# Routing of the first pair of batches moved behind GpSimd's last low part, and from GpSimd to VectorE

## The chip, the cores and the metric

The kernel runs on one core of a Trainium2 chip. The metric is the device time of one execution in microseconds (us); the median of several executions counts. PE is TensorE, DVE is VectorE, ACT is ScalarE, POOL is GpSimd, and SP issues most of the transfers.

## The reference

Three layers, in float32, one after the other:

```python
# attention: 4 batches, 8 heads, 576 positions, head size 64; each query sees itself and the 127 before it
scores = scale * q @ k.T  (masked to the window)  + slope[h] * -(i - j)
x = softmax(scores) @ v                               # -> 2304 tokens of 512
# mixture of 8 experts: each token goes to one
xn = x / (norm(x) + 1e-6);  en = emb / (norm(emb) + 1e-6)
logits = xn @ en.T / tau
expert = argmax(logits);  gate = softmax(logits)[expert]
x = gate * (relu(x @ w1[expert]) @ w2[expert])        # w1 512x1024, w2 1024x512
# dense layer, 512 -> 2048 -> 512, with a piecewise quadratic activation
out = g(x @ w_in) @ w_out
```

## The kernel before

The four batches are handled as two pairs (`pr` 0 and 1, `NP = 2`). A group `g` is one pair of batches and one pair of heads, eight in all (0 to 3 belong to the first pair of batches, 4 to 7 to the second); a group has nine units of 128 rows of queries, so the attention is 72 units. For a unit PE multiplies scores (`sc`, L862 to L867), DVE adds the bias and takes the maximum (`ss`, `mx`, L879), ACT takes the exponential (`at`, L887), PE transposes (`tp`, L894), ACT or DVE copies the transposed weights (`aT`, L899 or L901), and PE multiplies with the values (`av`, L914).

Queries and keys are split into a high part, made by ACT (`qs`, `kh`, L696 and L699), and a low part, made by DVE or POOL (`low`, L679; in groups 1 to 7 the planner chooses the engine). There are 16 splits, numbered 0 to 15, two to a group; PE's score matmuls need them.

Beside the attention run the steps of the routing. When the first pair's units are done, `route(0)` finds the expert of each token: the largest logit, its one-hot, running counts, the place of each token in its expert's list (`key`, `ki`, `lo`), then one-hots of these places in bf16 (`eqp`, `ocp`, `oap`, L403 to L412), which PE multiplies into the table of tokens (`tabp`, L420). From the table follow the expert that will be computed first (`efirst`), whose weights SP then loads (`wraw`), and its first token rows (`tabf`, L323), which POOL gathers from memory (`early_rows`, L565). `roots(0)` takes the root of the sums of squares of the first pair's tokens (`nsq` to `nrm`) by fifteen small operations after the two integer ones; on POOL before. `gates(0)` makes the gate weights from it (`inv`, L492, to `gfirst`, L323). With these ACT scales the gathered rows (L568), PE transposes them (`xpe`, L572), and they form the left side (`xte`) of the first expert's first 128 rows, which PE multiplies with unsplit weights (`hpe`, L1216) as soon as the attention ends. `route(1)` and `route(2)` do the same for the second pair.

The order of instructions on each engine is written by a planner when the program is built. Each step is a Python generator that yields an `ask`: the engines that could do it with assumed times, an earliest start, and names of events (`after`) that must have been seen. `drive` repeatedly takes the step with the earliest start on the planner's own clock. Events are kept in `seen` with planned times: `seen["split", n]` is the planned end of split `n`. An `after` moves a step in the order; it is no wait on the chip. There, each engine runs its instructions in the written order, and waits only for the data and buffers that an instruction uses. In planned idle time of PE the planner places small matmuls (`warm_up`, L815), whose results nobody reads. Arrival times of loads are planned by `arrival`.

After the attention come the experts (from L1455 on) and the dense layer, in which PE works without a break worth naming.

Of the kernel before, what the change touches and what calls it, by code (L numbers as in the profile page):

```python
# [15 lines left out]
ALU = mybir.AluOpType  # L16
# [4 lines left out]
P = 128  # L21
B, H, S, D = 4, 8, 576, 64
# [6 lines left out]
NT = 9  # L29
NP = B // 2  # L30
# [9 lines left out]
FILL, LEAST = 1.0, 0.45  # L40
TICK = 3.4133
EROOT = "G"
LATE = (0.4, 0.2, 0.5, 0.5, 0.2, 0.3)
OVER = (1, 3)
KEY = 4096
EVAC_DVE = (1, 3, 5, 7)
CT = CAP // P
# [13 lines left out]
def fused_kernel(ctx, tc, qk, vT, v, emb, tau, w1, w2, win64, wout64, out):  # L61
    nc = tc.nc
# [95 lines left out]
    seen, rings, work, held = {}, {}, {}, {}  # L158
    recent, warm, banks = [], [], []
    now, end, on, at_unit = [0.0], [0.0], ["", None], [0.0]  # L160

    def ask(engines, start=0.0, after=(), ring=None, late=None, duty=None, port=False):

        return engines, start, after, ring, late, duty, port
# [75 lines left out]
    def arrival(size):  # L240
        dma[0] = max(dma[0], end[0] + 0.65) + size / 0.35e6
        return dma[0] + 1.3

    rs_ = ExitStack()
    pr_ = rs_.enter_context(tc.tile_pool(name="pr", bufs=1, side="right"))
# [4 lines left out]
    nsq = pr_.tile([P, NQ], F32, name="nsq", bufs=1)  # L250
    nsq3 = pr_.tile([P, NQ], F32, name="nsq3", bufs=1)
    nrm = pr_.tile([P, NQ], F32, name="nrm", bufs=1)
# [78 lines left out]
    def vec(took=0.1, after=(), **k):  # L331

        return ask({"V": took}, end[0] + 0.13, after, port=True, **k)

    def of_tiles(what, c0, n):
        return [(what, q) for q in range(c0, c0 + n) if (q % NT) % 2 == 0]

    def route(i):
        c0, n = PARTS[i]
        pr, t0 = divmod(c0, NT)  # L340
# [4 lines left out]
        size = lambda m: 0.07 + m * n * E / 960  # L345
        lx = pr_.tile([P, n], F32, tag=f"lx{n}", name="lx")

        e, eng = ("V", nc.vector) if i else ("G", nc.gpsimd)
        yield ask({"V": size(1)} if i else {"G": 0.3}, after=of_tiles("lsum", c0, n) + ([] if i else [("enb", 1)]))
        if i == 0:  # L350

            eng.tensor_tensor(ls, ls, esc.rearrange("p (o e) -> p o e", o=1).to_broadcast(sh), op=ALU.mult)
            yield vec(size(1))
        nc.vector.tensor_reduce(lx, ls, axis=AX.X, op=ALU.max)
        if i == 0:
            seen["scaled"] = end[0]
# [4 lines left out]
        yield ask({e: size(1) if i else 0.15 + n * E / 474}, end[0] + 0.13, port=True)  # L361
        eng.tensor_tensor(fm, fm, wfirst[:, :n], op=ALU.mult)
        fl = pr_.tile([P, n], F32, tag=f"fl{n}", name="fl")
        yield vec(size(1))
        nc.vector.tensor_reduce(fl, fm, axis=AX.X, op=ALU.max)
        yield vec(size(1))
        nc.vector.tensor_tensor(oh[:, :, 1:], fm.rearrange("p t e -> p e t"),
# [31 lines left out]
        nc.vector.scalar_tensor_tensor(lo, ki, -float(P), key, op0=ALU.mult, op1=ALU.add)  # L399
        eq, oc, oa = eqp[:, t0:t0 + n], ocp[:, t0:t0 + n], oap[:, :, t0:t0 + n]  # L400
        ws = [P, n, NSLOT]
        yield ask({"V": size(CT)}, end[0], [("placed", 0)] if i else [])
        nc.vector.tensor_tensor(eq, slots(n, slotv), bc(ki, ws), op=ALU.is_equal)  # L403
        for t in range(n):
            yield ask({"V": 0.16}, end[0])
# [66 lines left out]
    def roots(pr):  # L472

        cols = slice(pr * NT, (pr + 1) * NT)
        e, eng = ("V", nc.vector) if pr else ("G", nc.gpsimd)
        yield ask({e: 0.08 if pr else 0.19}, after=of_tiles("squares", pr * NT, NT) + of_tiles("most squares", pr * NT, NT))
        eng.tensor_tensor(nsq[:, cols], nsq[:, cols], nsq3[:, cols], op=ALU.add)
        yield from root_steps(pr_, nrm[:, cols], nsq[:, cols], "p", e)
        seen["root", pr] = end[0] + 0.13

    def root_steps(pool_, out_, s_, nm, e):
        for n, _ in enumerate(root(pool_, out_, s_, nm, nc.vector if e == "V" else nc.gpsimd)):
            yield ask({"V": 0.08} if n < 2 or e == "V" else {"G": 0.19}, end[0] + 0.13, port=True)
# [94 lines left out]
    with ExitStack() as a:  # L578
# [38 lines left out]
        def qk_loads(n):  # L617
            g, b = divmod(n, 2)
            if n == 0:
                raw[0, 0] = new_raw()  # L620
                for c, cols in enumerate(CUT):
                    for x in range(2):
                        yield ask({"S": 0.45})
                        both = slice(2 * cols.start, 2 * cols.stop)
                        nc.sync.dma_start(raw[0, 0][:, x].rearrange("p h s -> p (h s)")[:, both],
                                          qk[0, 0, :, x].rearrange("p h s -> p (h s)")[:, both])
                        seen["qk"[x], 0, 0, c] = seen["qk"[x], 0, 1, c] = arrival(P * 8 * (cols.stop - cols.start) / 0.85)
                yield ask({"S": 0.45})
                nc.sync.dma_start(embt, emb)
                seen["emb"] = arrival(1e5) + 1.2  # L630
            else:
                yield ask({"S": 0.45}, after=[("loads", n - 1)] + ([("split", n - 3)] if n >= 3 else []))
                raw[g, b] = new_raw()
                pr, hp = divmod(g, H // 2)
                for x in range(2):
                    if x:
                        yield ask({"S": 0.45})
                    nc.sync.dma_start(raw[g, b][:, x], qk[2 * pr + b, hp, :, x])
                    seen["qk"[x], n] = arrival(P * 8 * S)
            seen["loads", n] = now[0]  # L640
# [109 lines left out]
        def prep_experts():  # L750

            esq = x_tiles[1][:E, 1]
            s_, g, y, t, o = (pa.tile([E, 1], F32, name=f"es{i}") for i in range(5))
            sub, e = (nc.vector, "V") if EROOT == "V" else (nc.gpsimd, "G")
            small = {e: 0.08 if e == "V" else 0.19}
            yield ask({"A": 0.52}, after=["emb"])
            nc.scalar.activation(esq, embt, AF.Square, accum_out=s_)
            yield ask({"V": 0.08}, end[0] + 0.2)
            nc.vector.tensor_scalar(y.bitcast(I32), s_.bitcast(I32), 1, None, op0=ALU.logical_shift_right)
            yield ask({"V": 0.08}, end[0] + 0.13)  # L760
            nc.vector.tensor_scalar(y.bitcast(I32), y.bitcast(I32), -1.0, 1597463007.0, op0=ALU.mult, op1=ALU.add)
            yield ask(small, end[0])
            sub.tensor_scalar(g, s_, -0.5, None, op0=ALU.mult)
            for _ in range(3):
                yield ask(small, end[0] + 0.13)
                sub.tensor_tensor(t, y, g, op=ALU.mult)
                yield ask(small, end[0] + 0.13)
                sub.tensor_tensor(t, t, y, op=ALU.mult)
                yield ask(small, end[0] + 0.13)
                sub.tensor_scalar(t, t, 1.5, None, op0=ALU.add)  # L770
                yield ask(small, end[0] + 0.13)
                sub.tensor_tensor(y, y, t, op=ALU.mult)
            yield ask(small, end[0] + 0.13)
            sub.tensor_scalar(y, y, s_, 1e-6, op0=ALU.mult, op1=ALU.add)
            yield ask(small, end[0] + 0.13, after=["tau"])
            sub.tensor_tensor(y, y, taut, op=ALU.mult)
            yield ask({"V": 0.08}, end[0] + 0.13)
            nc.vector.reciprocal(o, y)
            yield ask({"A": 0.2}, end[0] + 0.13)
            diag = pa.tile([E, E], F32, name="diag")  # L780
            nc.scalar.activation(diag, ident[:E, :E], AF.Copy, scale=o)
            ready = end[0] + 0.13
            yield ask({"P": 1.1}, ready, (), "xp", duty=0.1)
            etp = ps_x.tile([P, 5, E], F32, tag="xp", name="etp")
            for c in range(4):
                nc.tensor.matmul(etp[:, c], embt[:, c * P:(c + 1) * P], diag, start=True, stop=True)
            nc.tensor.matmul(etp[:, 4], one, diag, start=True, stop=True)
            yield ask({"V": 0.3}, end[0] + 0.2)
            for j in range(2):
                nc.vector.tensor_copy(enb[1][j * D:(j + 1) * D, :, j], etp[j * D:(j + 1) * D, :4])  # L790
            nc.vector.tensor_copy(esc, etp[:, 4])
            rings["xp"].append(end[0])
            seen["enb", 1] = end[0] + 0.13
# [126 lines left out]
        def finish(g, t, n, av, bank):  # L920
# [11 lines left out]
            if hp == H // 2 - 1:  # L932
                yield ask({"V": 0.2}, scaled, so_far("lpt"), late=LATE[0])
                nc.vector.tensor_reduce(lsum[:, q0:q0 + n], lpt[:, t:t + n].rearrange("p t h e -> p t e h"), axis=AX.X, op=ALU.add)
                seen["lsum", q0] = end[0] + 0.13
            xt = x_tiles[pr]
            yield ask({"V": 0.335, "A": 0.1 + 0.26 * n}, scaled, late=LATE[1])
            xo = xt[:, t:t + n, hp * P:(hp + 1) * P]
# [9 lines left out]
            if hp == H // 2 - 2:  # L948

                for i in range(n):  # L950
                    yield ask({"A": 0.59}, ready, so_far("xt"), late=LATE[2])
                    junk = p2.tile([P, 3 * P], BF16, tag="junk", name="junk", bufs=1)
                    nc.scalar.activation(junk, xt[:, t + i, :3 * P], AF.Square, accum_out=nsq3[:, q0 + i:q0 + i + 1])
                seen["most squares", q0] = end[0] + 0.13
            if hp == H // 2 - 1:
# [8 lines left out]
                for i in range(n):  # L964
                    yield ask({"A": 0.41}, ready, late=LATE[2] if pr == 0 else 0.0)
                    junk = p2.tile([P, 3 * P], BF16, tag="junk", name="junk", bufs=1)
# [689 lines left out]
```

## Time and profile before

| | |
|---|---|
| median of 3 runs | 828.44 us (828.44 to 829.73) |
| the profiled execution | 834.81 us, its span 833.1 us |
| granted TensorE clock, mean | 0.988 of full speed |
| busy: PE, DVE, ACT, POOL | 816.2, 518.8, 421.1, 141.0 us |
| instructions: PE, DVE, ACT, POOL | 5264, 1380, 881, 220 |
| end of the attention | about 175 us into the span |

A matmul counts as busy for as long as the records say that it is in the array, at the low clock for longer, and the placed matmuls without a reader count too. So PE's 98% is not all work: a stage can be shortened where PE is idle, where its clock is low, or where it runs such fill.

### The profile page before, as it was taken

The page shows a single profiled execution, that of the slowest core. Times are in us where ns is not written, and L with a number is a line of the kernel's source. Part 1 is how long each engine was busy: PE and PEld are TensorE (multiplying, and loading weights), DVE is VectorE, ACT ScalarE, POOL GpSimd, SP SyncE. Part 2 cuts the span into 40 slices and gives each one's busy share as a digit, 9 for nine tenths or more (in the row PEclk, how much of TensorE's full clock was granted, in tenths as well). Part 3 has the DMA queues.
Part 4 walks back from the last instruction along what each step waited for, and adds up shares of the span by engine and source line. Part 5 has one row for each costly group of instructions (what it writes and reads, how often), then busy time and mean ns, then how long its engine had stood idle before and what let it go on. Part 6 is the DMA issues. An engine that isn't in the chain of part 4 may idle for free.

```text
span 833.1 us, 14293 instructions
## 1 busy us (share of the span) xinstructions
PE 816.2 (98%) x5264; PEld 759.2 (91%) x5264; DVE 518.8 (62%) x1380; ACT 421.1 (51%) x881; POOL 141.0 (17%) x220
## 2 busy tenths in 40 slices
PE   8999998999999999999999999999999999999996
PEld 7999998987999999999999999999999999999995
DVE  6667785798666677787649999554434354334442
ACT  6878987765444376566435555333222233223222
POOL 3875856113101101100000000003000003001001
PEclk7999999899999999999999999999999999999999
DMA  8656956047746477678223343021000011001001
GB/s 297 239 184 228 335 221 233 27 144 220 238 137 193 149 268 251 225 246 260 73 67 134 119 137 113 1 77 76 1 1 1 1 39 76 1 1 39 1 1 38
DMA packets 59181, 106.04 MB, mean 127 GB/s; under 512 B 3942, under 2 KB 35686, under 8 KB 59104
## 3 DMA queue, kind: packets, MB, share of 16 engines
q1 hardware_dynamic: 55776, 95.15, 34.0%
q0 software_dynamic: 3328, 9.90, 3.4%
q8 instruction: 43, 0.70, 0.3%
q14 instruction: 34, 0.28, 0.1%
HBM read 90.42 MB, written 14.62 MB: 126 GB/s over the span
## 4 chain that ended last, share of the span: by engine, by line
issue 56%; PE 13%; POOL 2%; ACT 0%; POOLq 0%; DVE 0%
PE bh L1455 2%; POOL out L1581 2%; PE by L1444 2%; PE by L1446 2%; PE bh L1457 2%; PE by L1445 2%; PE bh L1456 2%; PE bx L1292 1%; POOL xg L1163 0%; POOL gap L1580 0%; PE permp L1382 0%; POOLq L1652 0%; ACT whi L552 0%; ACT yo L1494 0%; ACT xh L1284 0%
## 5 line engine op out<-in xcount | busy, mean ns | idle before, releaser
L1536 PE MATMUL ch<-yh,wc_0h 128*128 128x384 f32 x384 | 129.2, 336 | 0.0
L1538 PE MATMUL ch<-yh,wc_0l 128*128 128x384 f32 x384 | 129.1, 336 | 0.0
L1544 DVE SCALAR_TENSOR_TENSOR r<-r 128x384 f32<-128x384 f32 x96 | 53.4, 557 | 121.0 <-ACT r L1542 117.6
L1537 PE MATMUL ch<-yl,wc_0h 128*128 128x384 f32 x384 | 128.7, 335 | 0.0
L1542 ACT ACTIVATE r<-ch,halfc 128x384 f32<-128x384 f32 x96 | 55.3, 576 | 117.8 <-PE ch L1538 117.8
L1563 PE MATMUL o<-wc_1h,gl 128*128 128x512 f32 x288 | 113.3, 393 | 0.1
L1564 PE MATMUL o<-wc_1l,gh 128*128 128x512 f32 x288 | 113.3, 393 | 0.0
L1547 ACT ACTIVATE gh<-r 128x384 fp32r<-128x384 f32 x96 | 50.5, 526 | 123.4 <-DVE r L1546 123.4
L1562 PE MATMUL o<-wc_1h,gh 128*128 128x512 f32 x288 | 112.0, 389 | 0.0
L1581 POOL DMA_INDIRECT out<-ot,permu x18 | 17.5, 974 | 462.6 <-ACT ot L1576 459.6
L557 DVE TENSOR_TENSOR wlo<-wraw,whi 128x1024 fp32r<-128x1024 f32 x64 | 78.1, 1222 | 20.4 <-ACT whi L552 19.8
L1455 PE MATMUL bh<-xh,whi 128*128 128x256 f32 (+6 forms) x256 | 80.5, 314 | 0.4 <-issue 0.4
L1550 DVE TENSOR_TENSOR gl<-r,gh 128x384 fp32r<-128x384 f32 x96 | 53.4, 556 | 43.8 <-ACT gh L1547 42.6
L1445 PE MATMUL by<-hl,whi 128*128 128x256 f32 (+6 forms) x256 | 77.5, 303 | 1.9 <-DVE tmp L148 1.6
L1444 PE MATMUL by<-hh,whi 128*128 128x256 f32 (+6 forms) x256 | 77.5, 303 | 0.0
L1446 PE MATMUL by<-hh,wlo 128*128 128x256 f32 (+6 forms) x256 | 77.4, 303 | 0.0
L1457 PE MATMUL bh<-xh,wlo 128*128 128x256 f32 (+6 forms) x256 | 77.3, 302 | 0.0
L1456 PE MATMUL bh<-xl,whi 128*128 128x256 f32 (+6 forms) x256 | 77.1, 301 | 0.0
L1536 PEld LDWEIGHTS ch<-yh,wc_0h 128*128 128x128 f32 x384 | 72.1, 188 | 2.9 <-DVE r L1546 0.3
L1537 PEld LDWEIGHTS ch<-yl,wc_0h 128*128 128x128 f32 x384 | 72.1, 188 | 2.5
L1538 PEld LDWEIGHTS ch<-yh,wc_0l 128*128 128x128 f32 x384 | 72.0, 188 | 0.0
L887 ACT ACTIVATE at<-ss,mx 128x256 f32<-128x256 f32 (+1 forms) x144 | 60.1, 478 | 16.8 <-DVE mx L879 16.5
(277 smaller groups left out, 1748.6 us busy)
## 6 DMA issues: line engine op xcount, KB each, us to landing
wraw<-in_w SPq DMA_DIRECT2D x64, 512.0 KB, 4.4
rqk<-in_qk SPq DMA_DIRECT2D x30, 576.0 KB, 6.5
raw<-in_w_in SPq DMA_DIRECT2D x16, 512.0 KB
raw<-in_w_out SPq DMA_DIRECT2D x16, 512.0 KB, 4.6
vT<-in_vT SPq DMA_DIRECT2D x16, 288.0 KB
yl<-ysT SPq DMA_DIRECT2D x6, 768.0 KB, 5.9
x_dram<-xt SPq DMA_DIRECT2D x8, 512.0 KB, 6.5
vt<-in_v SPq DMA_DIRECT2D x8, 438.0 KB, 6.5
```

The source lines that it names most:

```text
L1444: nc.tensor.matmul(y, w2h[:, o], hh[:, :cap], start=(ff == 0), stop=False)
L1445: nc.tensor.matmul(y, w2h[:, o], hl[:, :cap], start=False, stop=False)
L1446: nc.tensor.matmul(y, w2l[:, o], hh[:, :cap], start=False, stop=(ff == 7))
L1455: nc.tensor.matmul(hp, w1h[:, o], xh[:, c, :cap], start=(c == 0), stop=False)
L1456: nc.tensor.matmul(hp, w1h[:, o], xl[:, c, :cap], start=False, stop=False)
L1457: nc.tensor.matmul(hp, w1l[:, o], xh[:, c, :cap], start=False, stop=(c == 3))
L1536: nc.tensor.matmul(hp, w1h[:, o], yh[:, c], start=(c == 0), stop=False)
L1537: nc.tensor.matmul(hp, w1h[:, o], yl[:, c], start=False, stop=False)
L1538: nc.tensor.matmul(hp, w1l[:, o], yh[:, c], start=False, stop=(c == 3))
L1562: nc.tensor.matmul(out_, gh[:, o], w2h, start=(ff == 0), stop=False)
L1563: nc.tensor.matmul(out_, gl[:, o], w2h, start=False, stop=False)
L1564: nc.tensor.matmul(out_, gh[:, o], w2l, start=False, stop=(ff == FF // P - 1))
```

## The change

The root of norms of the first pair runs on DVE, as that of the second pair does. The one-hots of `route(0)` and both `roots` may be planned only after `("split", 15)`, named `ALONE`, which is the planned end of the last low part. Where DVE takes up a result of POOL, the planner now leaves 1.0 us (`AFAR`) in place of 0.13 at three places. The planned arrival of the first group's loads is altered: without the factor 1/0.85, and 1.5 us later for the second of its two column halves (`c` is 0 or 1).

```diff
+AFAR = 1.0
...
+    ALONE = ("split", NP * H - 1)
+
     def route(i):
...
             eng.tensor_tensor(ls, ls, esc.rearrange("p (o e) -> p o e", o=1).to_broadcast(sh), op=ALU.mult)
-            yield vec(size(1))
+            yield ask({"V": size(1)}, end[0] + AFAR)
         nc.vector.tensor_reduce(lx, ls, axis=AX.X, op=ALU.max)
...
-        yield vec(size(1))
+        yield ask({"V": size(1)}, end[0] + (0.13 if i else AFAR))
         nc.vector.tensor_reduce(fl, fm, axis=AX.X, op=ALU.max)
...
-        yield ask({"V": size(CT)}, end[0], [("placed", 0)] if i else [])
+        yield ask({"V": size(CT)}, end[0], [("placed", 0) if i else ALONE])
         nc.vector.tensor_tensor(eq, slots(n, slotv), bc(ki, ws), op=ALU.is_equal)
...
     def roots(pr):
 
         cols = slice(pr * NT, (pr + 1) * NT)
-        e, eng = ("V", nc.vector) if pr else ("G", nc.gpsimd)
-        yield ask({e: 0.08 if pr else 0.19}, after=of_tiles("squares", pr * NT, NT) + of_tiles("most squares", pr * NT, NT))
-        eng.tensor_tensor(nsq[:, cols], nsq[:, cols], nsq3[:, cols], op=ALU.add)
-        yield from root_steps(pr_, nrm[:, cols], nsq[:, cols], "p", e)
+        yield ask({"V": 0.08}, after=of_tiles("squares", pr * NT, NT) + of_tiles("most squares", pr * NT, NT) + [ALONE])
+        nc.vector.tensor_tensor(nsq[:, cols], nsq[:, cols], nsq3[:, cols], op=ALU.add)
+        yield from root_steps(pr_, nrm[:, cols], nsq[:, cols], "p", "V")
         seen["root", pr] = end[0] + 0.13
...
-                        seen["qk"[x], 0, 0, c] = seen["qk"[x], 0, 1, c] = arrival(P * 8 * (cols.stop - cols.start) / 0.85)
+                        seen["qk"[x], 0, 0, c] = seen["qk"[x], 0, 1, c] = arrival(P * 8 * (cols.stop - cols.start)) + 1.5 * c
...
             sub.tensor_tensor(y, y, taut, op=ALU.mult)
-            yield ask({"V": 0.08}, end[0] + 0.13)
+            yield ask({"V": 0.08}, end[0] + AFAR)
             nc.vector.reciprocal(o, y)
```

Since the planner works from these numbers, the order moves in many places of the attention. Three of them follow; a line number of the changed kernel is 3 or 4 above that of the kernel before.

POOL, late in the attention, before the change: the gather of the first expert's rows stands ahead of the low parts of splits 14 and 15, and the sum of squares `nsq` and the first steps of the root behind them.

```order
L565 DMA xt_142<-x_dram,tabf 128x512
L679 TENSOR_TENSOR qs<-rqk,qs 64x512
L679 TENSOR_TENSOR kl<-rqk,kh 128x576
L679 TENSOR_TENSOR qs<-rqk,qs 64x512
L712 TENSOR_TENSOR qz_159<-rqk,qz_159 64x2x64
L679 TENSOR_TENSOR kl<-rqk,kh 128x576
L679 TENSOR_TENSOR qs<-rqk,qs 64x512
L679 TENSOR_TENSOR kl<-rqk,kh 128x576
L712 TENSOR_TENSOR qz_159<-rqk,qz_159 64x2x64
L679 TENSOR_TENSOR qs<-rqk,qs 64x512
L679 TENSOR_TENSOR kl<-rqk,kh 128x576
L477 TENSOR_TENSOR nsq<-nsq,nsq_102 128x9
```

The same low parts on POOL after the change, with what follows them.

```order
L682 TENSOR_TENSOR kl<-rqk,kh 128x576
L682 TENSOR_TENSOR qs<-rqk,qs 64x512
L682 TENSOR_TENSOR kl<-rqk,kh 128x576
L715 TENSOR_TENSOR qz_159<-rqk,qz_159 64x2x64
L568 DMA xt_142<-x_dram,tabf 128x512
L460 COPY oh_78<-cum_76 128x8
```

The gather has moved from ahead of these low parts to behind them, and nothing of the root is left on POOL.

DVE, late in the attention, before the change: the first integer step of the root (`rt_ip`), which takes POOL's `nsq`, stands among the maxima (`ss`, `mx`) of the units; the one-hots stand some eighty instructions earlier.

```order
L926 TENSOR_SCALAR rs<-av 128x4
L899 COPY aT<-tp 128x2x128
L928 RECIPROCAL rs<-rs 128x4
L879 ISA ss,mx<-sc,mb 128x256
L879 ISA mx 128x1
L124 TENSOR_SCALAR rt_ip<-nsq 128x9
```

DVE after the change, one unit later in the attention: the one-hots, and behind them the root in turn with the steps from the table.

```order
L902 COPY aT<-tp 128x512
L407 TENSOR_TENSOR eqp<-slotv,ki_all 128x216
L410 TENSOR_SCALAR ocp<-rowi,lo_all 128x128
L413 TENSOR_TENSOR oap<-eqp,tokhi 128x216
L410 TENSOR_SCALAR ocp<-rowi,lo_all 128x128
L416 TENSOR_SCALAR oap<-eqp,pid 128x216
L410 TENSOR_SCALAR ocp<-rowi,lo_all 128x128 x7
L929 TENSOR_SCALAR rs<-av 128x4
L480 TENSOR_TENSOR nsq<-nsq,nsq_102 128x9
L125 TENSOR_SCALAR rt_ip<-nsq 128x9
L931 RECIPROCAL rs<-rs 128x4
L127 TENSOR_SCALAR rt_yp<-rt_ip 128x9
```

What was spread over two places of the attention and over two engines now stands in one block on DVE, and no instruction in it takes a result of POOL.

DVE at the program's start, before the change: the low parts of the queries' second column half stand ahead of the first unit's maxima.

```order
L679 TENSOR_TENSOR kl<-rqk,kh 128x256 x2
L821 TENSOR_SCALAR mb<-rel 128x256
L679 TENSOR_TENSOR qs<-rqk,qs 64x256 x2
L879 ISA ss,mx<-sc,mb 128x128
L879 ISA mx 128x1
```

The same place after the change.

```order
L682 TENSOR_TENSOR kl<-rqk,kh 128x256 x2
L824 TENSOR_SCALAR mb<-rel 128x256 x2
L882 ISA ss,mx<-sc,mb 128x128
L882 ISA mx 128x1
L882 ISA ss,mx<-sc,mb 128x128
L882 ISA mx 128x1
L682 TENSOR_TENSOR qs<-rqk,qs 64x256
```

The first unit's maxima no longer stand behind the second column half.

## Rows read from the trace of the kernel before

**Rows 1.** Windows: length; busy PE, PEld, DVE, ACT, POOL; granted clock; DMA share, GB/s.
```profile
117.20:131.00 13.80, 13.52 (x137) 12.47 (x135) 11.45 (x58) 12.02 (x37) 4.39 (x5) 1.00 0.59 214
144.50:152.10 7.60, 7.60 (x42) 7.60 (x43) 4.25 (x20) 4.61 (x12) 3.09 (x14) 0.58 0.01 3
152.10:167.30 15.20, 15.14 (x161) 14.40 (x160) 12.35 (x67) 13.67 (x43) 0.00 (x0) 1.00 0.10 36
175.30:198.70 23.40, 21.32 (x138) 15.49 (x135) 21.55 (x97) 14.08 (x32) 8.71 (x8) 1.00 0.48 151
198.70:640.00 441.30, 439.79 (x2710) 415.64 (x2711) 294.43 (x541) 209.53 (x372) 21.32 (x29) 1.00 0.42 137
```

**Rows 2.** Timeline near 144 us: start, duration, engine, instruction, [idle before <-releaser].
```profile
143.59 0.21 POOL L477 TENSOR_TENSOR nsq<-nsq,nsq 128x9 f32<-128x9 f32 x1
143.84 0.17 DVE L124 TENSOR_SCALAR rt_ip<-nsq 128x9 int32<-128x9 int32 x1 [3.49 <-POOL nsq L477]
144.49 0.58 PE L866 MATMUL sc<-kh,qs 128*128 128x256 f32 x1 [3.44 <-DVE mx L879]
```

**Rows 3.** Timeline, 119 to 132 us: POOL, and the ACT instruction that it names.
```profile
119.18 1.52 POOL L679 TENSOR_TENSOR kl<-rqk,kh 128x576 fp32r<-128x576 f32 x1
126.49 1.24 POOL L565 DMA_INDIRECT xt<-x_dram,tabf  x1 [5.80 <-DVE tabf L323]
131.46 1.29 POOL L679 TENSOR_TENSOR qs<-rqk,qs 64x512 fp32r<-64x512 f32 x1 [3.73 <-ACT qs L696]
...
126.35 0.65 ACT L696 ACTIVATE qs<-rqk 128x512 fp32r<-128x512 f32 x1
```

**Rows 4.** Timeline of PE: ninth unit's eight score matmuls and what follows, at either clock.
```profile
124.96 0.36 PE L862 MATMUL sc<-kh,qz 128*128 128x256 f32 x1
125.98 1.90 PE L914 MATMUL av<-vt,aT 128*128 128x73 f32 x16
...
147.82 0.56 PE L862 MATMUL sc<-kh,qz 128*128 128x256 f32 x1
149.67 2.47 PE L914 MATMUL av<-vt,aT 128*128 128x73 f32 x16
```

**Rows 5.** Timeline, 119 to 127 us: DVE's one-hots and table, and PE beside them.
```profile
119.05 0.37 DVE L403 TENSOR_TENSOR eqp<-slotv,ki_all 128x216 bf16<-128x216 f32 x1
119.34 1.41 DVE L406 TENSOR_SCALAR ocp<-rowi,lo_all 128x128 bf16<-128x128 bf16 x1
122.03 0.72 DVE L406 TENSOR_SCALAR ocp<-rowi,lo_all 128x128 bf16<-128x128 bf16 x4
126.01 0.18 DVE L323 TENSOR_REDUCE tabf<-tm 128x3 uint32<-128x24 f32 x1
...
120.10 1.03 PE L815 MATMUL av<-warm 128*128 128x220 bf16 x9
121.70 1.32 PE L420 MATMUL tabp<-oap,ocp 128*128 128x24 bf16 x18
```

**Rows 6.** Timeline of the start, and a window of 1 us with the granted clock.
```profile
7.71 0.82 DVE L679 TENSOR_TENSOR qs<-rqk,qs 64x256 fp32r<-64x256 f32 x2 [1.63 <-ACT qs L696]
9.44 0.53 PE L894 MATMUL tp<-ident,at 128*128 128x128 f32 x2 [1.46 <-ACT at L887]
...
11.00:12.00 1.00, 1.00 (x8) 1.00 (x6) 0.54 (x2) 0.72 (x3) 0.00 (x0) 0.50 1.01 394
20.00:21.00 1.00, 0.94 (x5) 0.64 (x4) 1.00 (x2) 1.00 (x4) 0.00 (x0) 0.50 0.03 8
```

**Rows 7.** Timeline: second pair's root on DVE; first pair's gates; PE's transposes of early rows.
```profile
182.91 0.16 DVE L133 TENSOR_TENSOR rt_tp<-rt_tp,rt_yp 128x9 f32<-128x9 f32 x1
...
152.13 0.16 DVE L492 TENSOR_SCALAR inv<-nrm 128x9 f32<-128x9 f32 x1
161.37 0.18 DVE L323 TENSOR_REDUCE gfirst<-tm 128x3 f32<-128x24 f32 x1
...
162.68 0.60 PE L572 MATMUL xpe<-ident,xt 128*128 128x128 f32 x4
```

## The prediction

> **What bounds the kernel now.** I read the busy time by stage first, then the timeline of each engine wherever PE stands idle, runs fill or runs at the low clock. From 198.7 us on PE is busy for 439.79 of 441.3 us at full clock [rows 1], and the change touches nothing there but the names of tiles. So whatever the first 199 us gain or lose is carried to the end. In those, three losses of PE show.
>
> The largest stands at 144 us. DVE sits idle for 3.49 us in front of `rt_ip`, the first integer step of the first pair's root, until POOL has added the squares (`nsq`, 143.59); PE's next scores wait 3.44 us, since their banks are freed by DVE's maxima, which stand behind `rt_ip` [rows 2]. POOL was not slow at `nsq`; it was late, because the low parts of splits 14 and 15 stand ahead of it. And these were late because the gather of the early rows stands ahead of them: POOL waited 5.80 us for `tabf`, spent 1.24 us on the gather, and began the next low part only at 131.46. The wait of 3.73 us there is put down to ACT, but ACT's instruction began at 126.35 and took 0.65 us; what ended at 131.4 was, I take it, the gather's landing [rows 3].
>
> After that pause PE runs at the lower of its two levels. The stage from 144.5 to 152.1 us has a mean granted clock of 0.58 [rows 1], so about 0.42 / 0.5 of its 7.6 us, 6.4 us, at 1.2 GHz. Eight score matmuls take 1.85 us there (147.82 to 149.67), against 1.02 us at full clock (124.96 to 125.98) [rows 4].
>
> The second loss is at 119 us: the first bf16 one-hot takes 1.41 us, while four of its kind take 0.72 us together [rows 5]. It began while POOL worked at a low part (119.18, 1.52 us [rows 3]) and ended with it. PE is given 1.03 us of fill at this place [rows 5]. The third is at the start: PE idles 1.46 us before its first transposes, since the first maxima stand on DVE behind low parts whose data is still coming (1.63 us idle), and from 11 to 21 us the clock is at 0.50 [rows 6].
>
> **The change part by part.** The sum is made against the profiled execution, 834.81 us (span 833.1 and 1.7 around it). It lies 6.4 us above the median, and I carry the difference over to the median as it is.
>
> Pause at 144 us: no instruction of DVE's in this place takes a result of POOL any more, and the gather has left POOL's row ahead of the low parts. Minus 3.44 us. What is late next there is nothing that I see: PE has scores, transposes and values queued.
>
> Low clock behind it: at full clock the 6.4 us would take 6.4 x 1.02 / 1.85 = 3.5 us, a gain of 2.9. But ACT is busy for 4.61 us of this stage and DVE for 4.25 [rows 1]; 7.6 - 2.9 = 4.7 would leave ACT no gap. I take 2.4, with bounds of 0 (the clock falls for another reason) and 2.9.
>
> The stage from 117.2 to 131 us loses from PE the fill of 1.03 us, the table's matmuls of 1.32 us (which come back below) and 0.28 us of idle time, 2.6 us together. The order puts four fill matmuls into it, some 0.4 us by the nine in 1.03. ACT is busy for 12.02 of 13.8 us [rows 1], so that not over 1.8 can be had. I take 1.6, bounds 0.5 and 1.8.
>
> The block on DVE is the price. One-hots: from 119.05 to 122.75 us are 3.7 us; less 1.2 for the held one and 0.3 for a unit's own steps between them, 2.2 us. The steps from `table` to `tabf`: ten at about 0.17 (the last took 0.18 [rows 5]), 1.7 us. The root: twelve operations more than before, at 0.16 as those of the second pair [rows 7], 1.9 us. Together 5.8 us, put ahead of stage 152.1 to 167.3, in which DVE is busy for 12.35 of 15.2 us [rows 1] and so has 2.85 us free. About 3.0 us do not fit. The lower bound is 1.3: then all of it fits, since DVE has gaps in the stage ahead too (4.25 busy of 7.6), and PE alone has the table's 1.32 us more. The upper bound is 5.8, if nothing fits because the gaps are where DVE waits for PE. A part of this is a new wait: `nsq` on DVE needs ACT's last squares, and the table's steps and the next maxima are queued behind it. I take 3.0, nearest to the free time that the stage shows.
>
> That lateness goes no further by itself. Weights: SP reads `efirst` and issues six loads of 512 KB, which now start some 25 us later in the program; the stage 144.5 to 152.1 moves 3 GB/s and that to 167.3 moves 36 [rows 1], so that the path is free, and they are first used after 175 us. POOL's root steps were 3.09 us of work on an idle engine [rows 1], and their going gains nothing by itself. From 175.3 to 198.7 us DVE is busy for 21.55 of 23.4 us [rows 1]: the second pair's routing is its bound, with the same instructions as before, and it moves as a whole.
>
> The start: with the first maxima ahead of the second column half, most of the 1.46 us before PE's first transposes should go. I take 1.5. Bounds: a loss of 1 us, since the order has 31 short fill matmuls there instead of 39, and the clock could fall sooner; and a gain of 4.5, if PE stays at full clock through the ten us in which it now does not (10 x 0.45 by rows 4).
>
> The other two uses of `AFAR` and the rest of the reordering I cost at nothing: PE is at work nearly throughout there, and the planner puts other ready work in their place.
>
> Sum: -3.44 - 2.4 - 1.6 + 3.0 - 1.5 = -5.9 us, so 828.9 for a profiled execution and **822.5 us** for the median.
>
> **The rivals.**
>
> *The block does not fit.* DVE is the bound from 152 us on and the start gains nothing: -3.4 - 2.4 - 1.6 + 5.8 = -1.6, so 826.8 us. For it speaks that DVE's free 2.85 us are in pieces; against it that ACT (13.67 of 15.2 busy [rows 1]) sets many of these pieces and DVE can work ahead.
>
> *Slower: the gates come too late for the early rows.* Between `inv` (152.13) and `gfirst` (161.37, 0.18) lie 9.4 us [rows 7]. Ahead of `inv` now stand the one-hots, 2.2 us, and the root as a chain of fourteen steps, about 0.2 each with its hand-over, 2.8: 14.4 us from the block's start to `gfirst`. PE reaches the transposes of the early rows (162.68) 10.5 us after `inv` before the change; the order now has them two units later, 4 to 5 us at 175 us for 72 units, and the table's 1.3 ahead: about 16. So it is hidden by some 1.5 us, and turns when the block's 25 or so steps take 0.3 us in place of 0.2, 2.5 us more. Then ACT stands at the scaling of the early rows with the last units' exponentials behind it, PE waits in one piece, and its clock falls as at 144 us, 2.9. That is -1.6 + 2.5 + 2.9 = +3.8, so 832.2 us.
>
> *The low parts are not over when the one-hots come.* `ALONE` is an event on the planner's clock, and no wait on the chip. If POOL is still at splits 14 or 15, the change does not do what it says: each one-hot that meets a low part is held, by the first one's excess 1.41 - 0.18 = 1.2 us [rows 5]. Four meetings cost 4.9, -5.9 + 4.9 = -1.0, so 827.4 us. Against it: POOL was done at 143.6 with 9.5 us of waits around the gather [rows 3] that now go, and the block's place on DVE was reached at 152 us before. The Trainium skill (SBUF — State Buffer, "Who interferes with whom") has this as an exclusive lock on a port pair that VectorE and GpSimd share, held for a whole instruction, and counts VectorE operations with two SBUF inputs too. The held one-hot agrees. By that rule the root's steps on DVE, most of them with two SBUF inputs, could also be held, so that this rival could cost more than its four meetings; no row here shows such a step beside a low part.
>
> *The start gains its clock back.* 4.5 in place of 1.5: -8.9, so 819.5 us. For it: the maxima and the scores behind them come sooner, and the long run of fill at the start is planned among denser work. Against it: the loads still set the pace there, at 394 GB/s in the window at 11 us [rows 6].
>
> **How the numbers follow.** Forecast 0.52, block that does not fit 0.17, late gates 0.11, low parts not over 0.06, start at full clock 0.14. About 0.2%, 1.7 us, can be told from no change; the cases at 826.8 and 827.4 lie at that bound, and I count about half of each as no difference. Faster: 0.52 + 0.14 + half of 0.23, less some, 0.77; within 0.2%: 0.12; slower: 0.11. The forecast by itself spans 819.5 to 825.5. Range: 818 us (start at full clock and a block that mostly fits) to 828.5 (both cases near no change), which leaves out the late gates and little else.
>
> **What would show it.** Right: no wait of DVE for POOL in the last third of the attention; PE's clock at full from 130 to 175 us; the nine bf16 one-hots all near 0.2 us; POOL's last low part ahead of the one-hots; DVE near full from the one-hots to 199 us. The experts' unbroken stage, from 198.7 us on before, begins some 6 us earlier. Wrong: a wait of ACT for `gfirst` or of PE for the gates' matmuls of more than 1 us, a low clock near 160 us, a one-hot over 1 us, or a low clock at the start that lasts longer than the ten us of now.

## The result, and the profile after

The changed kernel takes **822.19 us** (median of 5 executions, 822.14 to 824.10), the kernel before beside it 829.73 (828.44 to 831.86): ratio 0.9912, 95% interval 0.9889 to 0.9936. Measured a second time (after_again, below) it is 0.9917 (0.9900 to 0.9934). So some 7 us less (7.5 between the medians, 6.9 by the second ratio), with 5.9 predicted, and inside the range.

The profiled execution of after takes 822.19, its span 820.5. That of before was 834.81, which turned out to be the slowest of some 60 executions of that kernel. So the two traces differ by 12.6 us and the medians by 7.5, and the difference has to be told apart by stage.

Windows of the changed kernel, with the columns of [rows 1]. The first covers the stage that had the low clock in [rows 6], the fourth the stage that had it in [rows 1].

```profile
10.00:20.00 10.00, 9.91 (x88) 9.48 (x87) 8.52 (x34) 8.71 (x21) 3.07 (x4) 1.00 1.03 407
20.00:30.00 10.00, 9.39 (x82) 9.00 (x80) 8.27 (x38) 9.83 (x23) 9.36 (x12) 1.00 0.85 327
117.20:131.00 13.80, 13.53 (x128) 13.00 (x127) 7.54 (x42) 12.52 (x35) 7.66 (x7) 1.00 0.10 31
140.00:150.00 10.00, 10.00 (x97) 9.55 (x97) 8.82 (x64) 9.46 (x32) 1.22 (x1) 1.00 0.55 184
150.00:160.00 10.00, 9.15 (x96) 8.32 (x96) 8.25 (x41) 9.01 (x27) 0.00 (x0) 1.00 0.58 210
160.00:170.00 10.00, 9.32 (x71) 7.74 (x71) 9.35 (x43) 8.76 (x31) 0.21 (x1) 1.00 0.56 190
187.40:640.00 452.60, 451.50 (x2775) 426.59 (x2776) 299.52 (x552) 212.56 (x379) 21.32 (x29) 1.00 0.42 134
```

The clock is at full in all of these windows. PE has gaps from 150 to 170 us, 1.5 us together, while the tail of the block is worked off. From 187.4 us on it is busy for 451.50 of 452.60 us, as before from 198.7 on.

Timeline of the changed kernel: PE's start, then POOL, DVE, ACT and PE around the block.

```profile
8.12 0.44 PE L897 MATMUL tp<-ident,at 128*128 128x128 f32 x2
11.26 0.36 PE L869 MATMUL sc<-kh,qs 128*128 128x256 f32 x1
...
120.30 1.28 POOL L682 TENSOR_TENSOR qs<-rqk,qs 64x512 fp32r<-64x512 f32 x1 [5.49 <-ACT qs L699]
133.36 1.44 POOL L682 TENSOR_TENSOR kl<-rqk,kh 128x576 fp32r<-128x576 f32 x1
136.53 0.46 POOL L715 TENSOR_TENSOR qz<-rqk,qz 64x128 fp32r<-64x128 f32 x1 [1.73 <-ACT qz L713]
143.77 1.22 POOL L568 DMA_INDIRECT xt<-x_dram,tabf  x1 [6.78 <-issue]
...
136.64 0.59 DVE L407 TENSOR_TENSOR eqp<-slotv,ki_all 128x216 bf16<-128x216 f32 x1
137.96 1.22 DVE L410 TENSOR_SCALAR ocp<-rowi,lo_all 128x128 bf16<-128x128 bf16 x7
139.17 0.16 DVE L480 TENSOR_TENSOR nsq<-nsq,nsq 128x9 f32<-128x9 f32 x1
144.31 0.16 DVE L495 TENSOR_SCALAR inv<-nrm 128x9 f32<-128x9 f32 x1
152.80 0.18 DVE L324 TENSOR_REDUCE gfirst<-tm 128x3 f32<-128x24 f32 x1
...
153.01 0.72 ACT L571 ACTIVATE xt<-xt,gfirst 128x512 f32<-128x512 f32 x1 [0.22 <-DVE gfirst L324]
153.82 0.62 PE L575 MATMUL xpe<-ident,xt 128*128 128x128 f32 x4
```

POOL's last long low part ends at 134.8, and only a short one (`qz`, to 136.99) meets the block; before, `nsq` could begin behind the last one only at 143.59 [rows 2]. No one-hot is held (seven in 1.22, against the 1.41 of one in [rows 5]); `nsq` stands behind them without a wait; ACT waits 0.22 for `gfirst`.

To compare executions by stage, four marks are read from each PE timeline: the first score of the ninth unit of group 0 (`sc<-kh,qz`), the same of group 5, the experts' first `bh` matmul (some 6 us ahead of their unbroken stage), and the span's end. The runs below are in this table; "old" and "new" say which order PE's instructions have up to the first mark.

| kernel | order of the start | to ninth unit, group 0 | to that of group 5 | to `bh` | to the end |
|---|---|---|---|---|---|
| before | old | 27.69 | 97.27 | 68.15 | 639.99 |
| start_only | new | 22.07 | 97.57 | 67.85 | 638.81 |
| root_dve | old | 25.84 | 97.36 | 64.14 | 638.66 |
| gather_late | old | 24.18 | 97.41 | 63.58 | 639.33 |
| gather_late_start | new | 22.08 | 97.30 | 62.63 | 638.89 |
| gather_late_after | new | 21.66 | 97.32 | 62.93 | 638.99 |
| onehots_late | old | 22.64 | 96.89 | 62.38 | 638.99 |
| start_old | old | 23.09 | 96.84 | 63.00 | 638.97 |
| root_pool_late | new | 21.84 | 97.04 | 62.55 | 639.77 |
| after | new | 21.86 | 97.02 | 62.97 | 638.65 |
| after_again | new | 21.15 | 96.98 | 63.01 | 638.96 |
| afar_old | new | 21.55 | 97.00 | 63.01 | 638.54 |
| pause_fill | old | 22.62 | 98.78 | 64.38 | 639.12 |
| onehots_twice | new | 22.32 | 96.99 | 66.61 | 639.28 |

Between the profiled executions of before and after, 5.8 us lie ahead of the first mark, 0.2 in the second column, 5.2 in the third and 1.3 in the last.

### The profile page after: what moved, and what is told of

The parts are those of the page before. It is cut to its first block, busy times and chain, and to the rows that moved or that the text cites. A ratio compares the mean times of both kernels' runs of the same rounds, so it can differ in the third digit from the quotient of the medians.

```text
span 820.5 us, 14256 instructions
## 1 busy us (share of the span) xinstructions
PE 806.9 (98%) x5242; PEld 749.8 (91%) x5242; DVE 516.9 (63%) x1390; ACT 421.5 (51%) x881; POOL 137.7 (17%) x205
## 4 chain that ended last, share of the span: by engine, by line
issue 56%; PE 12%; POOL 2%; ACT 0%; DVE 0%; POOLq 0%; ACTq 0%
PE bh L1458 2%; POOL out L1584 2%; PE bh L1460 2%; PE bh L1459 2%; PE by L1447 2%; PE by L1449 2%; PE by L1448 2%; PE bx L1295 1%; ACT whi L555 0%; DVE wlo L560 0%; POOL gap L1583 0%; PE permp L1385 0%; POOLq L1655 0%; POOL xg L1166 0%; ACT yo L1497 0%
## 5 line engine op out<-in xcount | busy, mean ns | idle before, releaser
L555 ACT ACTIVATE whi<-wraw 128x1024 fp32r<-128x1024 f32 x64 | 67.3, 1055 | 0.7 <-ACTq L1476 0.7
```

## The experiments

Each ratio is to the kernel before on the same chip (medians there 829.4 to 829.9), with its 95% interval. Two theories stood against each other after the result: that the late part gives 4.4 us and the start 1.5, as the prediction sums it, or that the start gives 4.5 to 6.

### The start apart from the rest

start_only takes the kernel before and this line of the change alone; start_old takes the changed kernel and undoes it.

```diff
-                        seen["qk"[x], 0, 0, c] = seen["qk"[x], 0, 1, c] = arrival(P * 8 * (cols.stop - cols.start) / 0.85)
+                        seen["qk"[x], 0, 0, c] = seen["qk"[x], 0, 1, c] = arrival(P * 8 * (cols.stop - cols.start)) + 1.5 * c
```

> The kernel before with the planned arrivals of the first loads alone changed; the routing stays as it was. Theory A (the sum of the prediction: the start is worth the idle time of 1.46 us): 1.5 us less than before, 829.7 to 828.2, ratio 0.998, and the ten us at the clock's lower level stay. Theory B (the changed kernel's trace read after the fact: the start gains its clock back): PE at full clock from 10 to 20 us, where before has 0.55, and 4.5 to 6 us less, ratio 0.993 to 0.995. Both expect the pause of about 3.4 us in front of the root's first integer step to stay.

> The changed kernel with the old planned arrivals of the first loads; the rest of the change stays. Theory A (the start is worth 1.5 us, the late part of the attention 4.4): 823.7, ratio to before 0.993, low clock again from 10 to 20 us. Theory B (the start is worth 4.5 to 6 us of the 7.5 that the medians differ by): 826.7 to 828, ratio 0.996 to 0.998. Both expect no wait of VectorE for GpSimd and full clock from 130 to 160 us.

start_only: **0.9985** (0.9976 to 0.9994), 827.97 us. start_old: **0.9935** (0.9921 to 0.9948), 823.49 us. Theory A holds in the times: 1.2 us for the start (1.6 between the medians), 5.4 for the rest. It is wrong on the low clock, which is not there in either trace; theory B has the clock of start_only right and the price wrong. Windows of start_only, start_old and root_dve (below), in this order; the last two have PE's old order at the start:

```profile
10.00:20.00 10.00, 9.91 (x89) 9.48 (x88) 8.61 (x32) 8.69 (x20) 3.34 (x4) 1.00 1.02 395
```
```profile
10.00:20.00 10.00, 9.72 (x89) 9.40 (x88) 8.19 (x29) 8.41 (x21) 3.01 (x4) 1.00 0.97 368
```
```profile
10.00:20.00 10.00, 9.94 (x61) 9.30 (x62) 6.67 (x22) 7.01 (x19) 0.47 (x2) 0.66 0.87 349
```

One order of instructions shows 1.00 in one execution, 0.66 in another, and 0.55 in the profiled one of before. PE's idle time ahead of its first transposes was 0.39, 0.88 and 1.46 us in these three. Over all six profiled executions with the old order the first mark lies between 22.62 and 27.69, over the eight with the new one between 21.15 and 22.32. So the low clock there belongs to some executions of the old order and not to all: it shows in three of the six, in none of the eight.

The pause stands as before in start_only, and the clock behind it is low; timeline, and a window:

```profile
138.53 0.17 DVE L124 TENSOR_SCALAR rt_ip<-nsq 128x9 int32<-128x9 int32 x1 [3.48 <-POOL nsq L477]
139.19 0.58 PE L866 MATMUL sc<-kh,qs 128*128 128x256 f32 x1 [3.43 <-DVE mx L879]
...
137.50:144.00 6.50, 4.81 (x23) 4.82 (x24) 3.39 (x16) 3.22 (x8) 4.07 (x16) 0.55 0.01 3
```

### The root on VectorE alone

root_dve: the kernel before, with the first pair's root on VectorE and no event to wait for.

```diff
-        e, eng = ("V", nc.vector) if pr else ("G", nc.gpsimd)
+        e, eng = "V", nc.vector
```

> The kernel before with the first pair's root on VectorE and nothing else: no event to wait for, the one-hots early, the gather still ahead of the last low parts on GpSimd. Theory W (what cost time was VectorE's wait for GpSimd's result): the pause of 3.44 us goes, the clock stays full from 140 to 160 us (2.4 us), up to 1.9 us of added steps come back: 4 to 5.8 us less, ratio 0.993 to 0.995. Rival L (two engines on one port): GpSimd is at low parts until 143.6 us, beside the root's steps on VectorE; each step that meets one is held for up to 1.2 us, so that three or four holds take the place of the pause and the clock falls again: within 1 us of before or slower, ratio 0.999 to 1.003, with single root steps above 1 us in place of 0.16.

**0.9969** (0.9953 to 0.9984), 826.89 us: 2.6 less, between the two. Timeline:

```profile
138.53 0.27 DVE L477 TENSOR_TENSOR nsq<-nsq,nsq 128x9 f32<-128x9 f32 x1
139.35 1.24 DVE L126 TENSOR_SCALAR rt_yp<-rt_ip 128x9 int32<-128x9 int32 x1
140.84 1.25 DVE L128 TENSOR_SCALAR rt_ip<-nsq 128x9 f32<-128x9 f32 x1
...
139.28 1.28 POOL L679 TENSOR_TENSOR qs<-rqk,qs 64x512 fp32r<-64x512 f32 x1
140.64 1.42 POOL L679 TENSOR_TENSOR kl<-rqk,kh 128x576 fp32r<-128x576 f32 x1
```

The pause is gone, and two steps of nine columns stand until the low part beside them ends: 1.2 us each in place of 0.17. The clock stays at 1.00. Both theories hold in part: taking DVE off POOL's result helps, and doing so while POOL is still late costs up to 2.2 us of it.

### One-hots late, root left on GpSimd; and the gather alone

onehots_late: the kernel before with `ALONE` ahead of the one-hots only. The gather takes its rows from the table that these make, so it moves behind the low parts with them (in the trace it starts at 145.51, the last low part at 137.20).

```diff
-        yield ask({"V": size(CT)}, end[0], [("placed", 0)] if i else [])
+        yield ask({"V": size(CT)}, end[0], [("placed", 0) if i else ALONE])
```

gather_late: the kernel before with the gather in `early_rows` behind the last low part, and nothing else; gather_late_start: that and the new arrivals.

```diff
-        yield ask({"G": 1.1}, after=["first rows", ("squares", 0), ("most squares", 0)] + of_tiles("out", 0, NT))
+        yield ask({"G": 1.1}, after=["first rows", ("squares", 0), ("most squares", 0), ("split", NP * H - 1)] + of_tiles("out", 0, NT))
```

> The kernel before with the event ahead of the first pair's one-hots alone; the root stays on GpSimd, which now has it right behind the low parts, and the gather behind that. Theory Q (GpSimd was late because of its queue, the gather ahead of the low parts): no wait of over 1 us for the sum of squares though it is still made by GpSimd, full clock from 130 to 160 us; 3.44 + 2.4 + 1.6 less, and 3.9 of one-hots and table steps against 2.85 free, 1.1 more: 6.3 us less, ratio 0.992. Rival H (the hand-over between the two engines is what costs): VectorE waits for GpSimd at the integer steps or at the inverse norms for 2 us and more, or one-hots beside GpSimd's root are held for over 1 us: 2 to 3 us less at the most, ratio 0.996 to 1.000.

> The kernel before with one thing changed: the gather of the first expert's rows is planned behind the last low part. One-hots early, root on GpSimd, start as before. Theory Q (the whole late gain is GpSimd's queue: the gather ahead of the low parts): pause 3.44 and low clock 2.4 go, nothing comes back on VectorE: 829.6 less 5.8, 823.8, ratio 0.993, no wait above 1 us for the sum of squares, full clock from 130 to 160 us. Rival O (the one-hots' place matters as much: the first one is held beside a low part, and PE runs fill there): at least 1.6 us less of the gain, 825.4 or more, ratio 0.995 and above.

> The kernel before with two edits: the gather planned behind the last low part, and the new arrivals of the first loads. One-hots early, root on GpSimd, no longer distance where VectorE takes up a result of GpSimd. Theory Q (these two are the whole change): 0.993 x 0.9985 = 0.9915, 822.8, as the changed kernel. Rival O (the late one-hots or the longer distance carry a part): 1 us or more above the changed kernel, 823.7 or more, ratio 0.993 and above.

onehots_late: **0.9934** (0.9921 to 0.9947), 823.17 us: 5.5 less, nearer to the 6.3 of its theory Q than to the 3 at most of rival H. gather_late: **0.9930** (0.9912 to 0.9948), 824.30. gather_late_start: **0.9935** (0.9920 to 0.9950), 823.32. Theory Q holds for gather_late: the edit to one line of `early_rows` gives 5.8 us (4.3 to 7.3 by the interval), as much as the late part of the change (5.4 by start_old), with the one-hots early and the root on POOL. Timeline of gather_late:

```profile
123.62 1.27 POOL L679 TENSOR_TENSOR qs<-rqk,qs 64x512 fp32r<-64x512 f32 x1 [6.46 <-ACT qs L696]
137.10 1.44 POOL L679 TENSOR_TENSOR kl<-rqk,kh 128x576 fp32r<-128x576 f32 x1
138.73 1.24 POOL L565 DMA_INDIRECT xt<-x_dram,tabf  x1 [0.19 <-DVE mx L879]
143.38 0.20 POOL L477 TENSOR_TENSOR nsq<-nsq,nsq 128x9 f32<-128x9 f32 x1 [3.41 <-ACT junk L967]
...
143.61 0.17 DVE L124 TENSOR_SCALAR rt_ip<-nsq 128x9 int32<-128x9 int32 x1
```

`rt_ip` no longer waits, though POOL makes `nsq`. With the gather ahead of it, that `qs` began 4.95 to 5.07 us after the gather's start in four traces (before, start_only, root_dve, pause_fill). In the written program of before it waits for `DMASW0`, the signal that the gather raises:

```
L565 DMA xt_142<-x_dram,tabf 128x512 [waits DMAHW4_49,DMAHW1_49,DMAHW6_49,DMAHW0_49,DVE_49]
L679 TENSOR_TENSOR qs<-rqk,qs 64x512 [waits DMASW0_49,PE_49,DMAHW6_49,Activation_49,Pool_49]
```

gather_late_start lies between its two theories: 823.32, where theory Q has 822.8 and rival O 823.7 or more. The intervals of 0.9935 and of the changed kernel's 0.9917 overlap. In the table it is 0.3 us longer than the changed kernel in the second column, where its table's matmuls still stand, and up to 0.4 shorter in the third: together nothing. Its six executions average 0.8 us above those of the changed kernel, which the experiments below take up. In gather_late the clock falls behind the table's matmuls, which are early there (pause_fill, below, has the same); window:

```profile
121.00:123.00 2.00, 2.00 (x12) 1.94 (x11) 1.52 (x12) 2.00 (x6) 0.00 (x0) 0.54 0.00 0
```

### Single parts of the change taken back

after_again is the changed kernel itself. gather_late_after is the changed kernel with the event of gather_late in `early_rows`, and the one-hots early again:

```diff
-        yield ask({"V": size(CT)}, end[0], [("placed", 0) if i else ALONE])
+        yield ask({"V": size(CT)}, end[0], [("placed", 0)] if i else [])
```

root_pool_late has the first pair's root on GpSimd again, behind `ALONE`, with the engine `eng` in the lines that follow; afar_old has the short distance.

```diff
+        e, eng = ("V", nc.vector) if pr else ("G", nc.gpsimd)
...
-AFAR = 1.0
+AFAR = 0.13
```

> The changed kernel with the first pair's one-hots back at their early place, and the gather alone planned behind the last low part; the root stays on VectorE behind the event, the start is the new one. By the prediction's terms: the stage from 117 to 131 us gives back 1.6, the block of 3.0 shrinks to the root's 1.9, which fits into the 2.85 us that are free: 1.4 us faster than the changed kernel, about 821.3, ratio to before 0.990. Rival N (the late block costs nothing, since it lies in gaps): 1.6 us slower than the changed kernel, about 824.3, ratio 0.9935.

> The changed kernel with the first pair's root on GpSimd again, behind the event. Theory Q (only GpSimd's queue mattered, not which engine takes the root): as the changed kernel within 0.1%, or up to 1.5 us less because VectorE has twelve steps fewer: 821 to 822.7, ratio to before 0.990 to 0.992. Rival E (the hand-over costs; the root belongs on VectorE): VectorE waits for GpSimd at the integer steps or at the inverse norms for over 1 us: 824 or more, ratio 0.9935 and above.

> The changed kernel itself, beside the others on one chip. Theory S (the parts add up): the start alone gave 0.9985, the rest without the start 0.9935, together 0.992, 822.9. Theory T (the start and the rest help each other, as the first ratio of 0.9912 with its wide interval would allow): 0.990 to 0.991, 821.3 to 822.1.

> The changed kernel with the old planned distance of 0.13 us at the three places where VectorE takes up a result of GpSimd. By the prediction, which costs them at nothing: as the changed kernel, 822.2 to 823.1, ratio to before 0.991 to 0.9925. Rival: VectorE stands at one of these three places for GpSimd, with a wait of 0.5 us and more in the trace, and 0.5 to 2 us more, ratio 0.993 to 0.994.

gather_late_after: **0.9931** (0.9910 to 0.9951), 822.92 us. root_pool_late: **0.9913** (0.9896 to 0.9930), 822.58. after_again: **0.9917** (0.9900 to 0.9934), 822.69. afar_old: **0.9926** (0.9911 to 0.9942), 822.59. Medians within 0.4 us: by them, where the one-hots stand, which engine takes the root, and the longer distance cannot be told from nothing once the gather is late. The means leave room for a small part of the one-hots' place: the twelve executions of gather_late_start and gather_late_after, with early one-hots, average 823.55, the 22 with late ones and the new start 822.62, 0.9 us less (0.3 to 1.6). Two of the twelve, at 825.03 and 825.89, make much of it; their mean clock is 0.997, that of the other four of gather_late_after 0.998 to 0.999, and no trace shows where it fell. The 1.4 us that the prediction's terms give gather_late_after over the changed kernel are not there. after_again lies nearer to theory S, and its interval holds theory T too.

The root on POOL is not quite without effect. PE's last values of the attention wait 0.97 us there, and from 161.5 to 168.5 us the mean clock is 0.76 (onehots_late, with the root on POOL too, has 0.98 us of waiting and 0.74 from 162 to 168.5). The changed kernel has 1.00 from 160 to 170. Timeline of root_pool_late:

```profile
162.51 1.12 PE L918 MATMUL av<-vt,aT 128*64 128x73 f32 x16 [0.97 <-ACT xt L946]
```

The times do not show what that costs, and to `bh` both are 0.4 to 0.6 us shorter than with the root on DVE.

### The clock behind the pause, and the block's price

pause_fill is the kernel before with 28 matmuls without a reader put into PE's pause, ahead of the scores of the unit that waits there:

```diff
+            if i == 61:
+                bank = [x for x, free in banks[-2:] if free <= busy["P"]][-1]
+                for _ in range(28):
+                    warm[0](bank)
```

onehots_twice is the changed kernel with each of the nine one-hots `ocp` of the first pair written twice:

```diff
             nc.vector.tensor_scalar(oc[:, t], rowi, lo[:, t:t + 1], None, op0=ALU.is_equal)
+            if i == 0:
+                nc.vector.tensor_scalar(oc[:, t], rowi, lo[:, t:t + 1], None, op0=ALU.is_equal)
```

> The kernel before with 28 short matmuls without a reader put on PE in the pause, ahead of the scores that wait for VectorE; 28 of 0.114 are 3.2 of its 3.44 us, and nothing else moves. Theory C (PE's low clock behind the pause follows from PE standing idle, and costs 2.4 us as the prediction has it): full clock from 140 to 160 us, the wait of VectorE for the sum of squares stays at 3.4, 829.7 to 827.3, ratio 0.997. Rival P (ScalarE and VectorE set the pace there, the clock costs nothing): full clock and no gain, ratio 0.9995 to 1.0005. Rival X (the clock falls for another reason): low clock as before, ratio 1.000.

> The changed kernel with each of the nine one-hots of the first pair's places written twice in a row, the same values: nine operations of 0.17, 1.5 us more in the block on VectorE. Theory B (the block lies on the path, as the prediction's term of 3.0 for what does not fit says: each further us costs a us): 1.5 us over the changed kernel, 822.7 to 824.2, ratio to before 0.9935. Rival G (the block lies in gaps of VectorE): within 0.4 us of the changed kernel, ratio 0.9915 to 0.992.

pause_fill: **0.9990** (0.9975 to 1.0005), medians 827.42 and 829.43: the times leave it open. Its timeline, and two windows of it:

```profile
137.42 2.88 PE L815 MATMUL av<-warm 128*128 128x220 bf16 x28
140.07 0.37 PE L870 MATMUL sc<-kh,qs 128*128 128x256 f32 x1
142.87 1.90 PE L918 MATMUL av<-vt,aT 128*128 128x73 f32 x16
...
139.32 0.17 DVE L124 TENSOR_SCALAR rt_ip<-nsq 128x9 int32<-128x9 int32 x1 [2.45 <-POOL nsq L477]
```
```profile
140.10:143.00 2.90, 2.90 (x29) 2.90 (x27) 2.45 (x11) 2.90 (x8) 2.08 (x10) 1.00 0.00 0
119.00:121.00 2.00, 2.00 (x12) 2.00 (x11) 1.50 (x11) 1.24 (x4) 0.00 (x0) 0.50 0.00 0
```

With fill in the pause the clock does not fall behind it, and the stage from the waiting scores to the `av` takes 140.07 to 142.87, 2.8 us, where it took 144.49 to 149.67, 5.2 [rows 2, 4]: the predicted 2.4. The wait of `rt_ip` is 2.45 us and not the 3.4 that were expected. And this execution lost its clock at 119 us, where nothing was changed, 1.4 us by the table's second column. How often that comes was not measured; the 12 executions, from 825.55 to 831.53, do not settle the gain.

onehots_twice: **0.9973** (0.9961 to 0.9985), 826.90 us, 4.2 over the changed kernel. Theory B, with a higher price. Timeline of PE, and a window:

```profile
140.93 0.21 PE L426 MATMUL tabp<-oap,ocp 128*128 128x24 bf16 x2 [0.24 <-DVE ocp L412]
...
143.60 0.56 PE L871 MATMUL sc<-kh,qs 128*128 128x256 f32 x1
```
```profile
143.40:147.40 4.00, 4.00 (x35) 3.70 (x33) 3.16 (x28) 3.25 (x12) 0.08 (x1) 0.65 0.00 0
```

I mis-sized the edit: the one-hots take 137.60 to 142.15 in it and 136.40 to 138.34 in after_again, 2.6 us more and not 1.5. The table's matmuls then wait for each one-hot, and the clock behind them falls to a mean of 0.65 for 4 us, 0.35 / 0.5 of them at the low level, which costs some 1.4. Together 4.0 of the 4.2 (3.6 in the table's third column). So a longer block lies on the path, and the changed kernel has little slack left there: its one-hots end at 139.18 and PE takes up the table's matmuls at 139.37. As the block stands it costs little, and the table shows the parts. The late one-hots shorten the second column by 0.3 us (97.30 and 97.32 in gather_late_start and gather_late_after, 96.98 to 97.02 in the changed kernel and afar_old) and leave the third within 0.1 (62.93 in gather_late_after, 62.97 to 63.01). The root on DVE lengthens the third by 0.3 to 0.6 (62.63 to 62.93, 62.55 to 62.97, 62.38 to 63.00).

## Why the prediction was right, step by step

**Pause and low clock, -3.44 and -2.4.** Right in cause, and in size as far as the runs tell: gather_late alone gives 5.8 by its ratio, gather_late_start is 5.5 shorter than start_only in the second and third columns, and pause_fill's trace shows the 2.4 apart. The chain as told (maxima behind `rt_ip`, that behind POOL, POOL behind the gather's landing) holds by the program's wait and by gather_late. What the text left undecided is which of two remedies does it. "No instruction of DVE's in this place takes a result of POOL any more" is not the reason: root_pool_late and onehots_late have such an instruction, `rt_ip` waits 0.27 us in them, and their times lose nothing. Taking it away with the gather left where it was gives 2.6 (root_dve). The reason is that the gather left POOL's row.

**Stage from 117 us -1.6, block +3.0.** Together +1.4 predicted; by gather_late_start and the changed kernel about 0 in the traces. Both terms are far off, and outside their bounds (0.5 to 1.8, and 1.3 to 5.8): taking the one-hots and the table out of the stage gives 0.3 us, the block costs 0.3 to 0.7. Their errors of 1.3 and some 2.5 us have opposite signs, so that the forecast came as near as it did partly by luck. The block fits: from 140 to 150 us PE is busy for all 10.00 us beside it, with fill only in the last one. Why the stage gives no more is not shown. The late part as a whole was predicted at -4.4; it is -5.4 in the traces (start_only to after, second and third columns) and -5.4 in start_old's ratio.

**Start -1.5.** 1.2 by start_only; 0.8 and 1.0 between the medians of start_old and after_again and of gather_late and gather_late_start. The rival that the start gains its clock back is what the two traces show, 5.8 us, and not what the medians do.

**Carrying the 6.4 us over "as it is".** This step failed. The sum gave 828.9 for a profiled execution, and it took 822.19, its median. Most of the 6.4 was the low clock at the start of that one execution: its first mark is at 27.69, the median of the six with the old order at 23.6. For the same reason the experts' unbroken stage began 11.3 us earlier in the trace (187.4 against 198.7), and not some 6. The median came out all the same since the start's term, 1.5, was taken from an idle time and not from the clock.

**The rivals.** Late gates: from `eqp` to `gfirst` 16.2 us and not 14.4, and still hidden, with 0.22 of waiting. Low parts not over: did not come here, since only `eqp` meets a last `qz` (0.59 against 0.37). root_dve shows such meetings: two root steps were held, by 1.1 us each. In it a step with two SBUF inputs (`nsq`) that met a low part (POOL, 137.34 to 138.78) took 0.27 us, from 138.53 to that part's end, and the long holds fell on two steps with one input, of the kind `tensor_scalar`. The Trainium skill (SBUF — State Buffer, "Who interferes with whom"), whose rule I had feared for steps with two SBUF inputs, also counts `tensor_scalar` among the operations that can take the shared ports. The trace agrees with it on both kinds of step. DVE is not near full up to the end of the attention, as I had it: 8.3 to 9.4 of ten us.

## What to carry to other kernels

Before moving work between engines because one waits for the other, look at what stands ahead of it in the late engine's row: here one indirect transfer, put behind ten low parts, gave within 1 us all that the late part of the larger change gave. A profiled execution is one draw: where its own time lies outside the timed ones, find the stage that makes it so before carrying its terms to the median.

## What was not expected of the hardware

- **The clock differs between executions of one order.** In the window from 10 to 20 us the old order had 0.55, 0.66, 0.94 and three times 1.00 in its six profiled executions; PE's idle time ahead of its first transposes was 1.46, 0.88 and 0.49 us in the first three, 0.39 and less in the others. Over 54 timed executions of the kernel before, the three fastest (826.51 to 826.78 us) have a mean clock of 0.996, the five slowest (831.65 to 831.98) 0.990. The changed kernel spreads less: 821.85 to 824.10 over 11 executions.
- **The clock can fall with no long pause of PE ahead.** Behind the table's short matmuls it fell in two of seven traces with early one-hots (0.50 and 0.54), in none of six with the plain late block, where PE does the eighteen in one run of 0.60 us, and in onehots_twice, where they wait for the one-hots. That these waits are the cause is not shown.
- **Nine columns can be held as long as 576.** Steps of 0.17 us took 1.24 and 1.25 beside low parts of 1.28 and 1.42.
- **The gather of 1.2 us closes POOL's row for 5.0**, while the instruction behind it waits for its queue. Why the program has that wait is not known from these runs, and no run leaves it out.
